# Whole strips for V in six one-layer steps at either end, half passes of 64 rows, and measured first times in the planner

## The chip, the core and the metric

The kernel runs on one core of a Trainium2 chip. Such a core has five engines with instruction queues of their own: TensorE (PE, matrix products; its weight loads are listed apart as PEld), VectorE (DVE), ScalarE (ACT), GpSimd (POOL) and SyncE (SP). SP and POOL also issue DMA transfers between the chip's memory and the core's on-chip memory. Work is ordered between engines with semaphores. The metric is the time of one execution on the device in microseconds; the number compared is the median over several executions.

## The reference

Two layers, each an attention with a recurrent memory followed by a gated feed-forward part, are applied twice with the same weights:

```python
x = x + A(layernorm(x)); x = x + B(layernorm(x))
x = x + A(layernorm(x)); x = x + B(layernorm(x))

def A(x):                               # 2048 rows of 512, 32 heads of 128
    mem = mem0                          # 8 rows
    for s in range(64):                 # segments of 32 rows, one after another
        h = concat(mem, x[32*s:32*s+32])            # 40 rows
        q, k, v = h @ Wq, h @ Wk, h @ Wv
        p = softmax(mask(q @ k.T * scale))
        o = (p @ v) @ Wo
        mem, out[s] = o[:8], o[8:]      # the first rows are the next segment's memory

def B(x):                               # F = 1792
    return (sigmoid(x @ w_gate) * (x @ w_up)) @ w_down
```

The memory makes the 64 segments of a layer a chain: segment s+1 can't start before the output projection of segment s is done. Inputs and outputs are bf16.

## The kernel before

Both attention layers run interleaved. Step t works on segment t of the first layer (j=0) and on segment t-6 of the second (j=1), side by side in one tile hT of 80 columns (`LAG` is 6). There are 70 steps. The first six have the first layer alone, the last six the second layer alone, with 40 columns; these are the one-layer steps. A feed-forward block works on four segments (128 rows, `BLK` is 4), and its pieces are spread between the attention work of the following steps.

One step (`emit_step`) goes through the 32 heads in six groups: Q and K (L834), a copy to on-chip memory by ACT, the scores (L848), the softmax on DVE and ACT (L862 to L879), transposes of P (L891), P times V (L914), and the output projection (L932), summed over all heads. Then DVE copies the new memory rows to the next step's hT (L945, L950), and ACT copies the rest to oxT, which L1002 transposes for the feed-forward block (L1034 gate and up, L1058 down).

V is not computed per step for all its rows:

- The rows of x of a segment that don't need the memory are known early. `v_pass` (L682) computes them for 128 rows at a time: 8 banks of 512 columns, four matmuls each, 32 matmuls of 128x512. The results go through a copy to the scratch tensor `scr` in the chip's memory. Before step 0 the first layer's passes come in groups (`v_group`), which is work for TensorE while the weights are loading. Later passes belong to the second layer and run after the feed-forward block that produces their rows; spare rows of those passes take up rows of the first layer (`v_fill`).
- The rows with the memory are computed in each step by `strips` (L759): 32 rows stand as a stationary tile of 32 columns, and four of them are put side by side in the array, 32 matmuls of 512 columns per strip.
- `emit_step` fetches both with SP DMAs into a tile `vsb`: L803 from `scr`, L814 from the strip's copy.

In the steps of `self.thin` a strip holds the memory and 24 rows of x, and only 8 rows come from `scr`. In the other steps 24 rows come from `scr` and the strip has the memory and 8 rows of x per layer. Before the change `thin` has four steps at either end; one-layer steps 4, 5, 64 and 65 are not in it.

The order of all instructions comes from a planner (`Planner`): every piece of work is a task with an engine, a duration, a latency, and keys that it reads and writes. `forward` runs through the tasks in a model of the engines, the PSUM banks and the DMA bus, and takes at each moment the ready task of highest priority. The priorities are not worked out in the kernel: they are a permutation written out as the string `SEQUENCE`. What is planned is emitted in order of planned start, engine by engine, so the planner's constants (`LAT`, `LEAD`, `TAIL`, `BUS`, `lat=`) and the string decide the instruction order, not the time at which an instruction runs on the chip. `warm` puts dummy matmuls (L1150) of a zero tile into planned holes of TensorE, so that its clock stays up; before `COLD` = 8000 ns of planned time it counts 1.2 columns per ns of the hole, after that 2.4. SP has eight DMA lanes: a DMA waits until the eighth one before it has landed. Large loads on POOL are also paced by TensorE's tasks.

At the start POOL clears tiles (L564 to L570), DVE and POOL normalise blocks of x (L638 to L642), TensorE transposes them (L651), and the first V matmul follows. Wv is loaded in five chunks of four or eight heads (L583), blocks of x between them (L721, L736).

Of the kernel before, what the change touches and what calls it, by code (L numbers as in the profile page):

```python
# [53 lines left out]
;AiJ8T3rAL|Nji^h>nE-)}}C6?#2*O0$8G4ZZdL%K2&sSfSGsr9F5bywiEpw1$9etJ{dj{n8$!UX!b>*%CVi0odWLR>PmMTURN8S`<`QSiresNn(7<<XH_|&hysZ(_+9io+E1yoPuJDs<%HrJ9~e&G  # L54
lO{?#YvSIBvP$R_;9f!1|GAlKk>X8^RhDlpmDnr7kt;6IZnSwn6|>@F3yW-VRO=#$!{s!|Z#sU*>kMf3XXFEnvc7`kKHK|1UA0@05#wb7a7HOlD?Yn#`J@z-(MeZ4Km`1|dy`f+^gMz@=%!FceG>$<
t$84$Kv|p6^^$~XKEw?)j1MY5bdV%#WrWw}B23to{C{XpW!a@PnfSMtcvtJ+x*0jL#Q{bGuEI}JeR4GK!d54vj>OKEncRQml~*<K;u1oaaQ4{bP`bof8*k|Jnvq^F=+Qyw{#`8!eH2|2^ft1nJbm7!
Ab!74vPh6M&l&LAlQ$kp(4RycR@9_lQx%SxC@=;7(#|M{pc-Zvq5^7mctV2pd4al%PqA<vseo$aQ(1$2O&p$$2=)#zF^2|o-u9XqFI-1Mc~jNaoYzdPrv`*zAA!u}T!KRNn7qKAo7WedWKFqAM5iWz
(lO=AI5ErprhTd6f)YVPYmhmHt`^X*krIWOe)K$vkW0fBn6t30v3~xgu9D9|2u?9Qhqxd3g!4-fxZSJdG?KXHi3=~m?P`o5>72)lIpD#^L81>xGR3Ji9|#WNB5L4{0_zR8rRp9-LS`%KDA3>to0^K8
trO%5X$z>-v_0tee?vxx^C`edFc{4p18&9J_1{77`WnlnpP=acza2)_2A~h&p}raH3Y3dS29jhXA=bf9kS8`f0IGrq5@}V)qI^z5??#c29baAb0B$86Cw+{B(m#uPRQTV>59ecM?f~YLiHK_agbl@M
>kXP60ej5O8Z1}7VtH~Tyi}o8Nh6os$k>dRMu$0U)mEux#MGAgPf!AyIq?@8yns1dXj`J(kB*bI#3S~kQG5MPNqKzX18+^sdBXNu6=5{T5Go1Hxs9?O$^vCQ9bSAntpCOL*N`Zy6d6f)8l}XGG}z!f  # L60
@(X9T<!k{a%zpTXjJr(t*vp+7A*WM2OF6JX&M0cCIFbCkn57sI8Q<FmQlDF2|3#N}6qtsBH%lb612z6V*1A9Y_A@HY$+fn$;9u1be-2ErQ~GLxg$2@V7S)+jTIXY3FAmgWqS`b0OT4UpsnQ7R$Uf33
f3q+HJ7f{+pc=}GM~NHQMP)4Ah>|J)wLO*-th<rKO_jdm{nOnoiY#EQdRE4_v%h|2_Nh`rzYRf!MHM6J(w85<_tb^)uriQo7uah{!`vFKpVnQ&1p}V2`ifjs&YA$@K)-I1;sCslWe)kvpEr4NIv$>b
$&(@1<pp8s;j>8S|K3v8wlu5u{sJg=#Rx9i+kw<LbAmj-UaSLL1MiR`VRCa!)$b@Ty6%s&&v4>}u`fQZ;+bdW<Ob3l-pr$_EMZQim=hbKvZ5di1HcO5lfzu>|J(t#K!!VbaFFOoH`q3<{|fuFn_mY>
# [90 lines left out]
class Task:  # L154
    __slots__ = ("eng", "dur", "lat", "fn", "deps", "succ", "tail", "boost", "ndep", "ready", "start", "idx", "on", "fresh", "acq", "rel", "durs", "tick", "prev", "land", "adj", "banks", "rate", "nb")

    def __init__(self, eng, dur, lat, fn, boost):
# [3 lines left out]
        self.acq, self.rel = [], []  # L161
        self.on = None
        self.land = 3000.0
        self.adj = {}
        self.banks = ()
        self.rate = 0.95
        self.nb = 0


class Buf:  # L170

    __slots__ = ("pool", "kind", "users", "first", "left", "slot", "t_free", "t_prev", "rd")

# [1048 lines left out]
```

## Time and profile before

| | |
|---|---|
| median of 4 runs | 1808.86 us (1807.73 to 1809.7) |
| the profiled execution, its own time | 1809.52 us |
| its span in the trace | 1807.8 us |
| busy: PE, DVE, ACT, POOL | 1771.7, 1152.5, 1189.5, 580.6 us |
| first V matmul of L682, first Q matmul of step 1 | 13.41, 89.07 us |
| end of the first six steps (the last copy of L950 before the two-layer steps) | 178.8 us |
| mean granted TensorE clock | 0.999 |
| data moved by DMA | 271.19 MB, mean 150 GB/s |

A row of the timeline reads: start, time from the first start to the last end of a merged group, engine, line, what it writes and reads, how many; in brackets the idle time of the engine before it and what ended it. Matmuls of TensorE overlap, so the price of one is the distance between starts and not its own duration. "L834 <- ACT qku" in the waits reads: the matmuls of line 834 waited for the ACT instruction that wrote qku. The chain that ended last is followed back from the last instruction; time on it is time that moves the end.

### The profile page before, as it was taken

The page shows a single profiled execution, that of the slowest core. Times are in us where ns is not written, and L with a number is a line of the kernel's source. Part 1 is how long each engine was busy: PE and PEld are TensorE (multiplying, and loading weights), DVE is VectorE, ACT ScalarE, POOL GpSimd, SP SyncE. Part 2 cuts the span into 40 slices and gives each one's busy share as a digit, 9 for nine tenths or more (in the row PEclk, how much of TensorE's full clock was granted, in tenths as well). Part 3 has the DMA queues.
Part 4 walks back from the last instruction along what each step waited for, and adds up shares of the span by engine and source line. Part 5 has one row for each costly group of instructions (what it writes and reads, how often), then busy time and mean ns, then how long its engine had stood idle before and what let it go on. Part 6 is the DMA issues. An engine that isn't in the chain of part 4 may idle for free.

```text
span 1807.8 us, 91891 instructions
## 1 busy us (share of the span) xinstructions
PE 1771.7 (98%) x39822; PEld 1524.9 (84%) x40039; DVE 1152.5 (64%) x3919; ACT 1189.5 (66%) x2987; POOL 580.6 (32%) x838
## 2 busy tenths in 40 slices
PE   9999999999999999999999999999999999999998
PEld 4588888988888888989898888988888888888886
DVE  4466665665566666665666667666666676566665
ACT  6666756676767666666766666666665666666664
POOL 6413032423233243323324241323334231332432
PEclk9999999999999999999999999999999999999999
DMA  9825254635455454445546463545556454554543
GB/s 344 274 71 151 58 150 117 192 110 155 141 160 151 131 169 142 142 129 160 159 128 197 129 179 91 167 139 163 153 145 178 120 142 119 157 153 126 178 124 109
DMA packets 136872, 271.19 MB, mean 150 GB/s; under 512 B 32650, under 2 KB 69138, under 8 KB 136466
## 3 DMA queue, kind: packets, MB, share of 16 engines
q0 software_dynamic: 56928, 184.07, 34.6%
q1 hardware_dynamic: 79538, 81.22, 15.7%
q8 instruction: 314, 5.14, 1.2%
q14 instruction: 92, 0.75, 0.1%
HBM read 220.93 MB, written 26.21 MB: 137 GB/s over the span
## 4 chain that ended last, share of the span: by engine, by line
PE 86%; DVE 7%; ACT 4%; issue 1%; POOL 1%; SPq 0%; ACTq 0%; DMA 0%; POOLq 0%; DVEq 0%
PE bank L834 30%; PE bank L932 15%; PE bank L1034 10%; PE bank L682 8%; PE bank L759 7%; PE bank L914 4%; PE bank L848 4%; PE bank L1058 4%; DVE st L862 2%; PE bank L891 2%; ACT ptsb L1158 1%; DVE small L867 1%; DVE small L874 1%; PE bank L651 1%; DVE st L869 1%
## 5 line engine op out<-in xcount | busy, mean ns | idle before, releaser
L834 PE MATMUL bank<-hT,wq_sb 128*128 128x80 bf16 (+1 forms) x8960 | 622.0, 198 | 0.9
L834 PE MATMUL bank<-hT,wk_sb 128*128 128x80 bf16 (+1 forms) x8960 | 621.9, 198 | 0.2 <-issue 0.2
L1158 ACT CAST qku<-bank 128x480 bf16<-128x480 f32 (+3 forms) x770 | 387.9, 513 | 220.0 <-PE bank L834 140.6
L834 PEld LDWEIGHTS <-wq_sb 128*128 128x128 bf16 x8960 | 454.9, 99 | 35.4 <-issue 22.1
L834 PEld LDWEIGHTS <-wk_sb 128*128 128x128 bf16 x8960 | 450.6, 99 | 0.1
L862 DVE TENSOR_TENSOR st<-bank,cst 40x240 f32<-40x240 f32 (+3 forms) x768 | 278.6, 367 | 233.0 <-PE bank L848 225.6
L932 PE MATMUL bank<-otsb,wo_sb 128*128 128x80 bf16 (+1 forms) x8960 | 363.3, 198 | 6.1 <-ACT otsb L1158 4.4
L932 PEld LDWEIGHTS <-wo_sb 128*128 128x128 bf16 x8960 | 338.0, 99 | 21.3 <-issue 8.1
L1026 POOL DMA_DIRECT2D wg<-in_B_w_gate_dram x217 | 164.4, 758 | 268.7 <-PE bank L1034 107.7
L1027 POOL DMA_DIRECT2D wu<-in_B_w_up_dram x217 | 163.9, 755 | 258.4 <-PE bank L1034 110.3
L1052 POOL DMA_DIRECT2D wd<-in_B_w_down_dram x217 | 153.7, 708 | 251.3 <-PE bank L914 82.4
L1158 ACT CAST otsb<-bank 128x480 bf16<-128x480 f32 (+3 forms) x420 | 198.0, 483 | 54.6 <-PE bank L914 40.8
L1158 ACT COPY ptsb<-bank 40x240 bf16<-40x240 bf16 (+3 forms) x559 | 177.9, 320 | 46.2 <-PE bank L891 36.5
L872 ACT ACTIVATE st<-st 80x240 f32<-80x240 f32 (+3 forms) x420 | 158.4, 381 | 43.5 <-DVE st L869 40.1
L1034 PE MATMUL bank<-xnT,wg 128*128 128x128 bf16 (+2 forms) x1784 | 171.5, 218 | 1.5 <-ACT xnT L1158 0.2
L1034 PE MATMUL bank<-xnT,wu 128*128 128x128 bf16 (+2 forms) x1784 | 171.0, 218 | 0.0
L874 DVE TENSOR_REDUCE small<-st 80x6 f32<-80x240 f32 (+3 forms) x420 | 151.3, 363 | 29.7 <-ACT st L872 27.3
L641 POOL TENSOR_TENSOR small<-small,cst 128x1 f32<-128x1 f32 (+1 forms) x80 | 45.2, 566 | 375.7 <-DVE small L640 357.4
L848 PE MATMUL bank<-qku 128*128 128x80 bf16 (+1 forms) x2240 | 160.5, 198 | 2.6 <-ACT qku L1158 1.5
L869 DVE TENSOR_TENSOR st<-st,small 80x240 f32<-80x240 f32 (+3 forms) x420 | 154.2, 369 | 3.5
L879 DVE TENSOR_TENSOR pb<-st,small 80x240 bf16<-80x240 f32 (+3 forms) x420 | 153.6, 369 | 4.1
L867 DVE TENSOR_REDUCE small<-st 80x6 f32<-80x240 f32 (+3 forms) x420 | 151.9, 363 | 4.5
(95 smaller groups left out, 2290.8 us busy)
## 6 DMA issues: line engine op xcount, KB each, us to landing
wg<-in_B_w_gate_dram POOLq DMA_DIRECT2D x220, 256.0 KB, 4.4
wu<-in_B_w_up_dram POOLq DMA_DIRECT2D x220, 256.0 KB, 4.3
wd<-in_B_w_down_dram POOLq DMA_DIRECT2D x220, 256.0 KB, 4.2
vsb<-scr SPq DMA_DIRECT2D x476, 48.0 KB
vsb<-sst SPq DMA_DIRECT2D x480, 32.0 KB
scr<-vst SPq DMA_DIRECT2D x120, 96.0 KB
wk_sb<-in_A_Wk_dram SPq DMA_DIRECT2D x10, 384.0 KB
wq_sb<-in_A_Wq_dram SPq DMA_DIRECT2D x10, 384.0 KB
```

Source lines behind the costliest of these rows:

```text
L834: nc.tensor.matmul(o_ap, lhsT=W[:, c, h * P:(h + 1) * P], rhs=mv(c), start=(c == 0), stop=(c == DC - 1))
L848: nc.tensor.matmul(s_all(SB)[:, w0 + i, :], lhsT=fview(qku[:, i, 0, 0:1], [(1, P)]), rhs=qku[:, i, 1, 0:ncol], start=True, stop=True)
L862: pl.add("DVE", dve_ns(n, True), lambda gsz=gsz, hs=hs, st=st, SB=SB, pj_=pj_, npj_=npj_, mk=mk, idx=idx: nc.vector.tensor_tensor(out=st[p ...
L867: pl.add("DVE", dve_ns(n), lambda hs=hs, st=st, mx=mx: nc.vector.tensor_reduce(out=mx[pr, hs], in_=st[pr, hs], axis=AX.X, op=ALU.max), r=s ...
L869: pl.add("DVE", dve_ns(n), lambda gsz=gsz, hs=hs, st=st, mx=mx: nc.vector.tensor_tensor(out=st[pr, hs], in0=st[pr, hs], in1=mx[pr, hs].uns ...
L872: pl.add("ACT", act_ns(n), lambda hs=hs, st=st: nc.scalar.activation(out=st[pr, hs], in_=st[pr, hs], func=ACTF.Exp, scale=self.scale), r=s ...
L874: pl.add("DVE", dve_ns(n), lambda hs=hs, st=st, sm=sm: nc.vector.tensor_reduce(out=sm[pr, hs], in_=st[pr, hs], axis=AX.X, op=ALU.add), r=s ...
L932: nc.tensor.matmul(WB[:, c * ncol:(c + 1) * ncol], lhsT=self.wo[:, h, c * P:(c + 1) * P], rhs=otsb[:, hl, 0:ncol], start=(h == 0 and c == ...
L1026: pl.add("POOL", 760, lambda wg=wg, fs=fs: nc.gpsimd.dma_start(out=wg[:], in_=self.wgv[:, :, fs]), r=[("wo", self.H - 1)], w=[gk] + bt, la ...
L1027: pl.add("POOL", 760, lambda wu=wu, fs=fs: nc.gpsimd.dma_start(out=wu[:], in_=self.wuv[:, :, fs]), r=[("wo", self.H - 1)], w=[uk] + bt, la ...
L1034: nc.tensor.matmul(gu[:, 2 * i + k, 0:n], lhsT=W[:, c, i * P:(i + 1) * P], rhs=xnT[:, c, rw], start=(c == 0), stop=(c == DC - 1))
L1158: nc.scalar.copy(out=dst, in_=src)
```

## The change

- `thin` goes from four steps at either end to six, which are all the one-layer steps. Steps 4, 5, 64 and 65 now take the memory and 24 rows from the strip and 8 rows from `scr`.
- So fewer rows are needed in `scr`. Of the first layer's blocks 0 and 1, block 0 needs 8 rows of each segment, and block 1 needs 8 rows of each segment and 16 more of two of them. One pass of 128 rows (`v_group([0, 1], ...)`) becomes one strip set (`v_strip`) and one half pass (`v_half`). For the second layer's block 14 (`b == NBLK - 2`) a pass becomes a half pass.
- `v_half` is new: 64 rows stand as a stationary tile of 64 columns, two beside each other in the array, 32 matmuls of 512 columns for all heads.
- At the program's start, blocks 2, 14, 3, 4, 5, 7 come ahead of mem0, block 0 and block 1.
- Wv is loaded in eight chunks of four heads, each after the chunk two before it has landed; the first chunk is issued before any block of x.
- The planner's constants change: a first time per engine (`FIRST`), lead times per queue, a slower bus in the first 18 us, and shorter latencies of transfers.
- A fourth buffer for the small results of the layernorm (`lns`).
- `SEQUENCE` is a new permutation, so the order of instructions differs on every engine and in nearly every step.

```diff
-    BUS, LEAD, TAIL, BIG, ROOM, POOL0 = 345.0, 2000.0, 1900.0, 300000, 1.0, 2000.0
+    BUS, BUS0, SLOW, BIG, ROOM, TAIL = 345.0, 290.0, 18000.0, 300000, 1.0, 1200.0
+    LEAD = {"SP": 1000.0, "POOL": 1800.0}
+    FIRST = {"PE": 0.0, "ACT": 2040.0, "DVE": 980.0, "POOL": 3500.0, "SP": 750.0}
...
-        free = {"PE": 0.0, "ACT": 0.0, "DVE": 0.0, "POOL": self.POOL0, "SP": 0.0}
+        free = dict(self.FIRST)
...
-                    bus = max(bus, now + self.LEAD) + tk.nb / self.BUS
+                    bus = max(bus, now + self.LEAD[e])
+                    bus += tk.nb / (self.BUS0 if bus < self.SLOW else self.BUS)
...
-        for h0, n in ((0, 4), (4, 4), (8, 8), (16, 8), (24, 8)):
+        for h0, n in ((0, 4), (4, 4), (8, 4), (12, 4), (16, 4), (20, 4), (24, 4), (28, 4)):
             cs = slice(h0 * P, (h0 + n) * P)
-            ld(self.wv[:, :, cs], wv_v[:, :, cs], P * self.DC * n * P * 2, [("wv", h) for h in range(h0, h0 + n)])
+            tk = ld(self.wv[:, :, cs], wv_v[:, :, cs], P * self.DC * n * P * 2, [("wv", h) for h in range(h0, h0 + n)], [("wv", h0 - 8)] if h0 > 4 else [])
+            if h0 > 4:
+                tk.after = pl.writer[("wv", h0 - 8)]
...
+    def take_part(self, pst, B, j, tile, keys, c0, r0, n, i0):
+
+        off = r0 + (MEM if j else 0) + SEG * i0
+        dst = fview(tile[:, 0, c0:c0 + 1], [(P, self.DC), (n, 2), (1, n)])
+        self.pl.add(("ACT", "DVE"), copy_ns(8 * n, True),
+                    lambda: (dst, fview(pst()[:, 0, off:off + 1], [(P, self.DC), (SEG, 2), (1, n)])), r=[B], w=keys)
+
+    def v_half(self, tile, c0, keys, j, b, q8, r16, i16, boot=False):
+        ...
+        for s in range(2):
+            vb = [pl.buf(self.bank, "v"), pl.buf(self.bank, "v")]
+            def mm(s=s, vb=vb):
+                for q in range(2):
+                    for c in range(DC):
+                        for i in range(2):
+                            k = 4 * s + 2 * i + q
+                            nc.tensor.matmul(vb[q][64 * i:64 * i + 64, :], lhsT=tile[:, c, c0:c0 + 64], rhs=self.wv[:, c, k * 512:(k + 1) * 512],
+                                             start=(c == 0), stop=(c == DC - 1), skip_group_check=True)
...
+    def v_strip(self, cols, keys, j, b, q8):
+        sb = self.strips(cols, keys)
...
-r=[("vd", j, b, q, kk) ...], w=[("vx", j, vh, i)], lat=5000.0, nb=nx * 2048)
+r=[("vd", j, b, q, kk) ...], w=[("vx", j, vh, i)], lat=4300.0, nb=nx * 2048)
...
-r=[(sb, 0), (sb, 1)], w=[(name, j, vh, i)], lat=3500.0, use=[sb], nb=nr * 2048)
+r=[(sb, 0), (sb, 1)], w=[(name, j, vh, i)], lat=3200.0, use=[sb], nb=nr * 2048)
...
+            if b == self.NBLK - 2:
+                self.take_v(pst2, B2, 1, self.xvl[q], [("xvl", q, 0)], 0, 16, 8)
+                self.take_part(pst2, B2, 1, self.xvl[q], [("xvl", q, 1)], 32, 0, 16, 0)
+                self.write_hT_x(pst2, B2, 1, BLK * b + self.LAG)
+                self.v_half(self.xvl[q], 0, [("xvl", q, 0), ("xvl", q, 1)], 1, b, 2, 0, 0)
                 return
...
-        self.thin = (range(BLK), range(self.NSEG - BLK, self.NSEG))
+        self.thin = (range(self.LAG), range(self.NSEG - self.LAG, self.NSEG))
...
-        p0 = self.pre1(0)
-        p1 = self.pre1(1)
...
-        self.load_mem0()
         self.load_weights()
...
-        self.v_group([0, 1], {0: p0, 1: p1}, [[(0, 96, 0, 8)], [(0, 0, 0, 24)]])
         self.v_group([2, 14], {}, [[(0, 0, 0, 24)], [(0, 96, 0, 8)]])
         self.v_group([3, 4, 5, 7], {}, cuts)
+        self.load_mem0()
+        p0 = self.pre1(0)
+        p1 = self.pre1(1)
+        x0 = self.xvl[2]
+        self.take_v(*p0, 0, x0, [("xvl", 2, 0)], 0, 0, 8)
+        self.v_strip(lambda c: x0[:, c, 0:32], [("xvl", 2, 0)], 0, 0, 0)
+        self.take_v(*p1, 0, x0, [("xvl", 2, 1)], 64, 0, 8)
+        self.take_part(*p1, 0, x0, [("xvl", 2, 1)], 96, 8, 16, 2)
+        self.v_half(x0, 64, [("xvl", 2, 1)], 0, 1, 0, 8, 2, True)
         self.v_group([8, 10, 11, 13], {}, cuts)
```

The latency of the feed-forward weights' loads goes from 5200 to 4700 in the same way. `v_half` ends with two copies and four DMAs per `s` to `scr`; `v_strip` ends with four DMAs.

## The prediction

> **What bounds the kernel now.** I read the page first (shares, then the chain that ended last), then the busy time by stretches of 5 us and of 100 us, then the timeline of TensorE in the head, TensorE's waits, and last the end of the chain.
>
> ```profile
> PE 1771.7 (98%) x39822; PEld 1524.9 (84%) x40039; DVE 1152.5 (64%) x3919; ACT 1189.5 (66%) x2987; POOL 580.6 (32%) x838
> PE 86%; DVE 7%; ACT 4%; issue 1%; POOL 1%; SPq 0%; ACTq 0%; DMA 0%; POOLq 0%; DVEq 0%
> ```
>
> TensorE is the bound: 98% busy, 86% of the chain. By stretches (start:end, then PE, PEld, DVE, ACT, POOL busy, clock, DMA share, GB/s):
>
> ```profile
> 5.00:10.00 5.00, 3.00 (x18) 1.16 (x16) 2.90 (x8) 1.30 (x4) 3.91 (x15) 0.96 0.93 305
> 40.00:45.00 5.00, 5.00 (x25) 2.29 (x24) 0.00 (x0) 3.20 (x6) 1.32 (x3) 1.00 1.05 366
> 100.00:105.00 5.00, 4.25 (x111) 3.40 (x108) 2.57 (x14) 2.95 (x11) 0.67 (x1) 1.00 0.24 69
> 1000.00:1100.00 100.00, 98.37 (x2238) 87.42 (x2249) 65.77 (x220) 65.63 (x161) 32.71 (x45) 1.00 0.52 150
> ```
>
> There are three stages. In the head, to about 80 us, TensorE and the DMA are both full. In the one-layer steps TensorE has holes, some of them stopped with dummy matmuls (L1150). In the two-layer steps TensorE is full and nothing else is near its limit. So V work taken out pays in the head and in the middle, and only partly in between. The head on the timeline, start and duration first:
>
> ```profile
> 1.00 5.44 PE L1150 MATMUL bank<-hot 128*128 128x512 bf16 x13 [1.00 <-DVE cst L557]
> ...
> 9.00 0.40 PE L651 MATMUL bank<-cst,xn 128*128 128x128 bf16 x4 [2.00 <-DVE xn L642]
> 9.23 3.21 PE L1150 MATMUL bank<-hot 128*128 128x512 bf16 x8
> ...
> 13.41 1.04 PE L682 MATMUL bank<-wv_sb,xvf 128*128 128x512 bf16 x4
> ...
> 60.81 2.75 PE L682 MATMUL bank<-wv_sb,xvf 128*128 128x512 bf16 x12
> 63.40 0.31 PE L848 MATMUL bank<-qku 128*128 128x40 bf16 x6
> ...
> 87.23 1.91 PE L759 MATMUL bank<-wv_sb,hT 128*32 128x512 bf16 x32
> 89.07 0.27 PE L834 MATMUL bank<-hT,wq_sb 128*128 128x40 bf16 x4
> ```
>
> Prices come from the distance between starts. A whole V matmul takes (63.40-60.81)/12 = 0.216 us. A strip matmul (32 columns, four side by side) takes (89.07-87.23)/32 = 0.0575 us. The first dummies take 0.43 us each: the array ran at half speed. Step 1 begins at 89.07. What TensorE waited for from 200 to 1600 us (us in total, times, longest):
>
> ```profile
> PE bank L1002 <- ACT oxT L1158: 4.6, 10, 0.5
> PE bank L932 <- ACT otsb L1158: 2.5, 6, 0.7
> PE bank L848 <- ACT qku L1158: 0.7, 2, 0.5
> ```
>
> No DMA stands there. The end of the chain, start and duration, dummies alone:
>
> ```profile
> 1792.02 0.38 PE bank L1150 x2
> ...
> 1792.77 0.92 PE bank L1150 x4
> ...
> 1794.37 0.27 PE bank L1150 x2
> ...
> 1796.00 0.48 PE bank L1150 x2
> ```
>
> **The change part by part.** The code's new SEQUENCE reorders every engine. I compared the instruction orders of the two programs.
>
> *V work.* 64 whole V matmuls go (13.8 us). In come 32 strip matmuls (1.84 us) and 64 half matmuls of 64 columns, two abreast. Nothing in the trace shows a half. Its ends are 0.108 (half of 0.216, perfect overlap) and 0.216 (none); I take 0.111, near the low end, because the strips overlap four ways at 0.0575 against an ideal 0.054. A use of 32 halves is then 3.55 us. In the head one pass (6.9) becomes a strip set and a half pass (1.84+3.55): -1.5. In the middle block 14's pass becomes a half pass: -3.4 (0 if the halves do not overlap).
>
> The Trainium skill, "TensorEngine Tiling (Array Packing)", Key Properties, speaks against this: changing the tiling mode drains the array. The strip rows hold such switches already, and 32 strips cost 1.84 against 32 x 0.054 = 1.73, so at most 0.11 a stretch. With four stretches of halves and two more sets of strips that rule would turn the sum below from -5.7 to about -5.1.
>
> *First dummies.* The program opens with 12.5 dummies of 512 columns now, with 31.5 after. They then separate three groups of transposes with 8.75, 3.75 and 2.75 more. The first V matmul follows. At 0.43 us until about 6.2 (in the trace the dummies are at full speed from 6.55) 12 run; the other 19.5 at 0.216 end at 10.4. Three transpose groups at 0.23 and 15.25 dummies at 0.216 (3.3) follow: V starts at 14.4, against 13.41. Ends: all 31.5 slow, 18.4; data first, 12.1 (the first normalised block can reach TensorE at about 8.1: two memsets of 0.44 fewer stand ahead of POOL's first L641, which starts at 7.34 now, 1.66 before its block is at TensorE).
>
> "TensorE: Matmul & The Clock Gate", Part 1, has the array at half clock until a free-running window of 3.4 us was busy. By it the turn falls between 4.4 and 7.8 us, the dummies end between 9.5 and 11.2 and V starts between 13.5 and 15.2. The trace agrees as to the size (slow to about 6.1), and shows a relapse to half clock at 10 to 13 us, after the 2.00 us wait, that the longer fill would avoid.
>
> *Rest of the head.* Between V's start and step 1 the order has 256 whole V matmuls now and 216 after: 32 are the pass that becomes strips and halves, and eight move past step 1's start. Work now: 55.3 V + 3.7 strips + 6.4 QK + 3.2 L932 + 2.0 scores, transposes and PV + 2.0 transposes of L651 + 0.7 dummies = 73.3, in 75.7 us, so 2.4 idle. After: 46.7 + 3.55 + 5.5 + 6.4 + 3.2 + 2.0 + 2.1 = 69.45, with the same idle 71.9. Step 1 begins at 14.4 + 71.9 = 86.3, that is **-2.8**, with ends -5.1 and +1.2 from V's start alone.
>
> This needs the weights in time. The load is the same (16.8 MB of weights, x, about 8 MB of V written), and the DMA runs at 366 GB/s from 10 to 70 us. Now the last L932 weights are issued by 75 us and used from 84. The cover is thus some 5 us, and the change uses 2.8 of it. SP's queue gets 19 more DMAs, POOL's 12 fewer; V writes now stand on SP from its 22nd DMA on, and each waits for an ACT copy with the weights of Wq, Wk and Wo queued behind it. Were the cover gone, the price is the 2.8. Wv's eight chunks wait for the second one before; SP's queue has a limit of eight in flight anyway, so this adds nothing that the queue didn't do.
>
> *One-layer steps.* Steps 4, 5, 64 and 65 fetch 8 rows instead of 24 from scratch and 32 instead of 16 from the strip, in the same number of strips, with as many DMAs. SP issues these, and TensorE doesn't wait for them now. Cost 0; ends -2.0 (dummies of steps 1 to 5 fall by that) and +1.7 (the eight V matmuls that moved there; they lie in holes: 4.25 of 5 us busy at 100).
>
> *Middle order.* Where the closing L932 of a step is followed at once by L1002, TensorE waits for ACT's oxT copy, up to 0.5 us. The order has 4 such places now and 7 after: **+1.5**. With the half pass the middle gives **-1.9**, ends -10 (all listed waits gone too) and +10 (below).
>
> *End.* After the last L932 1.8 us of dummies fall to 0.2, work of L1034 and L1058 in their place. They lie on the chain (2.05 us above), but what they wait for may stay: **-1.0**, between -2.0 and 0.
>
> Sum: -2.8 + 0 - 1.9 - 1.0 = **-5.7**. The profiled execution took 1809.5 (span 1807.8), 0.66 above the median of 1808.86. So 1803.8 by its own time and **1803.2** as a median. A difference within 0.2%, 3.6 us, is what a measurement here can't tell from none.
>
> **Rivals.**
> 1. *Slower: transfers planned too tight.* The plan now counts V reloads 0.7 us shorter (5.0 to 4.3), FFN weights 0.5, strips 0.3. The order may put the first PV of a step that much nearer to its reload. One place, L914 behind the vsb loads of L803, in 58 two-layer steps: more than 5.7/58 = 0.1 us a step takes the gain, 0.25 us a step gives +14.5-5.7, 1812. Against it: no DMA in TensorE's waits now, and the weights land in a median 4.4 us. Chance 0.16.
> 2. *The head pays nothing.* Dummies slow for longer, or V writes on SP hold the weights back: then -2.9 or less is left, 1806. Halves that do not overlap end here too (-5.7+6.7, 1810). Chance 0.20.
> 3. *Better than the sum.* The new order also removes the listed waits of the middle and the dummies of steps 1 to 5: -12, 1797. Against: its places with short cover are as many as before. Chance 0.14.
>
> **How the numbers follow.** The forecast has 0.50, with 1800 to 1806 as its own range. Faster by over 0.2% (below 1805.2): most of the forecast (0.44), rival 3, a little of rival 2: 0.61. Same: 0.06 of the forecast and most of rival 2: 0.23. Slower: 0.16. The range goes from just under rival 3 to the price of rival 1: 1795 to 1812.
>
> **What will show it.** The first L682 at 14 to 15 us; the first L834 of step 1 near 86; L682's whole matmuls 64 fewer and halves 0.11 us apart; L1002 waiting 6 to 7 us for oxT; about 0.2 us of dummies after the last L932. I am wrong if TensorE's waits name L914 with vsb transfers, if the head shows waits for weights, or if halves stand 0.216 apart.

## The result, and the profile after

The changed kernel takes 1813.06 us (median of 42 executions, 1809.92 to 1816.19) against 1810.3 for the kernel before (60 executions, 1807.67 to 1813.5). The ratio is 1.0015 with a 95% interval of 1.0011 to 1.0019. It is slower by 0.15%, which lies inside the 0.2% that the prediction called no difference, though the interval leaves no change out. The forecast of 1803.2 was faster by 0.31%. The measured time lies 9.9 us above it and 1 us above its range; 1.5 us of the 9.9 are the reference, whose median was 1808.86 us over 4 executions and is 1810.3 over 60.

The profiled execution took 1811.38 us, with a span of 1809.4 (before: 1807.8). The page's shares, then the chain that ended last:

```profile
PE 1770.8 (98%) x39846; PEld 1523.6 (84%) x40067; DVE 1164.2 (64%) x3931; ACT 1182.0 (65%) x2971; POOL 574.1 (32%) x826
PE 82%; DVE 7%; ACT 5%; issue 3%; DMA 2%; SPq 1%; POOL 1%; ACTq 0%; POOLq 0%; DVEq 0%
```

TensorE is the bound as before, at 98%. But its share of the chain fell from 86% to 82%, and DMA, which had 0%, has 2% (about 36 us). Four transfers of the head, before 61 us, make 25 of them: the chain now runs through transfers there. The same stretches as before (start:end, then PE, PEld, DVE, ACT, POOL busy, clock, DMA share, GB/s):

```profile
5.00:10.00 5.00, 5.00 (x24) 2.14 (x22) 3.29 (x8) 2.53 (x2) 2.62 (x8) 1.00 0.98 323
40.00:45.00 5.00, 4.81 (x25) 2.17 (x24) 0.00 (x0) 1.08 (x3) 0.00 (x0) 1.00 1.06 342
100.00:105.00 5.00, 4.74 (x127) 3.75 (x124) 4.26 (x20) 4.51 (x18) 1.11 (x2) 1.00 0.40 121
1000.00:1100.00 100.00, 98.33 (x2230) 87.32 (x2238) 66.79 (x226) 65.06 (x159) 33.85 (x47) 1.00 0.52 150
```

In the first row the clock reads 1.00 where it read 0.96: the kernel before fell back to half clock at 9.63 us, and this one did not. (The share covers only what is on record. The first clock record of this trace begins at 5.59 us, and before it the dummies start 0.43 us apart.) In the second ACT is busy for 1.08 us where it was busy for 3.20 us before, with TensorE still nearly full. The head on TensorE's timeline (start, duration, line, what, how many; in brackets idle time and what ended it). V's passes are now L690, halves L727, strips L812, Q and K L887, dummies L1210:

```profile
1.00 9.22 PE L1210 MATMUL bank<-hot 128*128 128x512 bf16 x32 [1.00 <-DVE cst L563]
...
14.16 1.90 PE L690 MATMUL bank<-wv_sb,xvf 128*128 128x512 bf16 x7
...
19.89 1.92 PE L727 MATMUL bank<-wv_sb,xvl 128*64 128x512 bf16 x16
21.75 0.60 PE L690 MATMUL bank<-wv_sb,xvf 128*128 128x512 bf16 x2
...
56.66 1.03 PE L690 MATMUL bank<-wv_sb,xvf 128*128 128x512 bf16 x4
61.00 7.48 PE L690 MATMUL bank<-wv_sb,xvf 128*128 128x512 bf16 x27 [3.32 <-ACT wg L1218]
...
88.81 1.91 PE L812 MATMUL bank<-wv_sb,hT 128*32 128x512 bf16 x32 [0.30 <-issue]
90.66 0.27 PE L887 MATMUL bank<-hT,wq_sb 128*128 128x40 bf16 x4
```

V starts at 14.16 where 14.4 was forecast. 16 halves take 21.75 - 19.89 = 1.86 us, so 0.116 apiece: two columns of the array do work side by side. Then TensorE stands for 3.32 us at 57.7, and the 27 matmuls after that take 7.48 us, where 27 at 0.216 would be 5.8: the granted clock is half from 60.21 to 63.62. Step 1 begins at 90.66 instead of the forecast 86.3, and 1.6 later than the 89.07 of before. TensorE's waits from 200 to 1600 us (us in total, times, longest):

```profile
PE bank L1055 <- ACT oxT L1218: 4.6, 11, 0.5
PE bank L985 <- ACT otsb L1218: 1.1, 5, 0.3
...
PE bank L901 <- ACT qku L1218: 0.5, 2, 0.3
```

L1055 (before L1002) waits as long as before, 4.6 us, and L985 (before L932) less. Nothing in this view accounts for a loss. At the end one dummy is left after the last output projection of L985, as forecast:

```profile
1792.02 0.96 PE L985 MATMUL bank<-otsb,wo_sb 128*128 128x40 bf16 x32
...
1796.22 0.33 PE L1210 MATMUL bank<-hot 128*128 128x384 bf16 x1
```

### Where the time came from

The ends of the same steps in the two profiles give the difference by stage. Each column but the forecast is one profiled execution, and each number says by how many us that stretch took longer than in the profile before. Stretches are named by their times in the kernel before. The columns from e2 on are kernels of the experiments below and stand here because all are read in the same way.

| stretch | forecast | after | e2 | e5 | e8 | e3 | e6 | e9 |
|---|---|---|---|---|---|---|---|---|
| head, to 87.1 | -2.8 | +1.0 | -3.6 | -4.1 | -2.8 | +2.6 | -3.9 | -4.5 |
| one-layer steps and three more, 87.1 to 256.6 | 0 | +1.5 | +2.4 | +3.8 | +2.5 | +3.5 | +3.8 | +1.0 |
| 256.6 to 1466.8 | +1.5 | +4.3 | +5.1 | +4.9 | +3.8 | +0.4 | +0.5 | -0.2 |
| 1466.8 to 1595.7 | | -0.9 | -0.9 | -0.8 | -0.9 | -0.3 | -0.3 | -0.4 |
| block 14, 1595.7 to 1695.6 | -3.4 | -2.3 | -2.4 | -2.1 | -2.3 | -0.9 | -1.7 | -2.1 |
| end, from 1695.6 | -1.0 | -1.9 | -1.0 | -1.9 | -1.8 | -0.1 | +0.4 | -1.5 |
| sum | -5.7 | +1.7 | -0.4 | -0.2 | -1.5 | +5.2 | -1.2 | -7.7 |

Three terms failed: the head, the one-layer steps and the middle. The experiments take them in turn. A profile is one execution. That of the kernel before is 0.8 us faster than its median, that of the changed kernel 1.7 faster, that of e2 1.2 slower. e4 and e10 below keep the head of the kernel before and still stand at +1.0 and +0.9 there, with half clock for 6.83 us where its profile has 3.41. So the columns tell where time goes, to about 1 us in the head, and the ratios below tell how much in all.

### The stall in the head

The wait of L690 at 57.7 is for ACT (a copy to the buffer wg). ACT's waits from 10 to 90 us, and its timeline at the two places:

```profile
ACT wg L1218 <- DMA scr<-wg: 6.8, 1, 6.8
ACT wu L1218 <- DMA scr<-wu: 5.7, 1, 5.7
```

```profile
36.88 1.31 ACT L1218 CAST wd<-bank 128x512 bf16<-128x512 f32 x2
43.92 0.59 ACT L1218 CAST wu<-bank 128x512 bf16<-128x512 f32 x1 [5.73 <-DMA scr<-wu]
...
52.93 0.59 ACT L1218 CAST wg<-bank 128x512 bf16<-128x512 f32 x1 [0.28 <-PE bank L690]
60.37 0.59 ACT L1218 CAST wg<-bank 128x512 bf16<-128x512 f32 x1 [6.85 <-DMA scr<-wg]
```

In the kernel before, ACT's waits over the same stretch name a write out of a staging buffer only once:

```profile
ACT wg L1158 <- DMA scr<-wd: 0.3, 1, 0.3
```

In the head V's results go to `scr` through staging buffers. The idle weight buffers wd, wg and wu serve as nine of them, 1024 columns each, filled in two halves by two groups of matmuls and copies. ACT waits here for the earlier write out of the same buffer: the one behind 60.37 was issued at 53.49 and landed at 60.27. The banks of TensorE fill up behind ACT until it stands as well.

The plan did not see this. `Planner` counts a buffer as taken from its first-listed user (`T[bf.users[0]].acq.append(bf)`), which is the first half's group. For these two buffers the sequence runs the second half's group first, 11.0 and 12.6 us ahead in planned time. So on the chip the buffer is wanted that much earlier than the plan believes, before the write out of it can have landed.

### The profile page after: what moved, and what is told of

The parts are those of the page before. It is cut to its first block, busy times and chain, and to the rows that moved or that the text cites. A ratio compares the mean times of both kernels' runs of the same rounds, so it can differ in the third digit from the quotient of the medians.

```text
span 1809.4 us, 91920 instructions
## 1 busy us (share of the span) xinstructions
PE 1770.8 (98%) x39846; PEld 1523.6 (84%) x40067; DVE 1164.2 (64%) x3931; ACT 1182.0 (65%) x2971; POOL 574.1 (32%) x826
## 4 chain that ended last, share of the span: by engine, by line
PE 82%; DVE 7%; ACT 5%; issue 3%; DMA 2%; SPq 1%; POOL 1%; ACTq 0%; POOLq 0%; DVEq 0%
PE bank L887 29%; PE bank L985 15%; PE bank L1087 9%; PE bank L812 7%; PE bank L690 6%; PE bank L967 4%; PE bank L901 4%; PE bank L1111 3%; PE bank L944 2%; ACT ptsb L1218 2%; DVE st L915 1%; ACT qku L1218 1%; DVE small L927 1%; PE bank L1210 1%; DVE small L920 1%
## 5 line engine op out<-in xcount | busy, mean ns | idle before, releaser
L887 PE MATMUL bank<-hT,wq_sb 128*128 128x80 bf16 (+1 forms) x8960 | 622.1, 198 | 0.7 <-issue 0.2
L887 PE MATMUL bank<-hT,wk_sb 128*128 128x80 bf16 (+1 forms) x8960 | 621.8, 198 | 0.1
L887 PEld LDWEIGHTS <-wq_sb 128*128 128x128 bf16 x8960 | 454.5, 99 | 35.9 <-issue 24.7
L887 PEld LDWEIGHTS <-wk_sb 128*128 128x128 bf16 x8960 | 450.6, 99 | 0.2
L985 PE MATMUL bank<-otsb,wo_sb 128*128 128x80 bf16 (+1 forms) x8960 | 364.8, 198 | 3.7 <-ACT otsb L1218 1.9
L985 PEld LDWEIGHTS <-wo_sb 128*128 128x128 bf16 x8960 | 339.0, 99 | 21.8 <-issue 5.8
L1218 ACT COPY ptsb<-bank 40x240 bf16<-40x240 bf16 (+3 forms) x577 | 182.5, 318 | 40.9 <-PE bank L944 30.8
L649 POOL TENSOR_TENSOR small<-small,cst 128x1 f32<-128x1 f32 (+1 forms) x80 | 44.6, 559 | 410.4 <-DVE small L648 410.0
L932 DVE TENSOR_TENSOR pb<-st,small 80x240 bf16<-80x240 f32 (+3 forms) x420 | 154.0, 370 | 4.9
```

Source lines behind the costliest of these rows:

```text
L887: nc.tensor.matmul(o_ap, lhsT=W[:, c, h * P:(h + 1) * P], rhs=mv(c), start=(c == 0), stop=(c == DC - 1))
L985: nc.tensor.matmul(WB[:, c * ncol:(c + 1) * ncol], lhsT=self.wo[:, h, c * P:(c + 1) * P], rhs=otsb[:, hl, 0:ncol], start=(h == 0 and c == ...
L1218: nc.scalar.copy(out=dst, in_=src)
```

## The experiments

Each ratio is against runs of the kernel before in the same session, whose median was 1811.9 us for e1 to e4, 1811.79 for e5 to e8 and 1810.02 for e9 and e10. So the ratios can be compared with each other and with the 1.0015 of the changed kernel, and the times of different sessions cannot.

Two theories stood against each other for the head: SP's queue (the prediction's rival 2, writes of V that hold weights back) and the staging buffers. For the middle the question was whether its order or something carried over from the head costs the time.

### e1: writes of V on the other queue

All of the head's V writes and loads that may go on either queue go to POOL, so that none stands on SP ahead of weights.

```diff
-                    {"SP": nc.sync, "POOL": nc.gpsimd}[tk.on].dma_start(out=got[1], in_=got[2])
+                    (nc.gpsimd if len(tk.durs) > 1 else nc.sync).dma_start(out=got[1], in_=got[2])
```

> The changed kernel with one edit: all V writes of the head (L1214) go on POOL's queue, so that no weight on SP stands behind a write that waits for ACT. Queue theory: in the changed kernel SP issued nothing from 41.9 to 47.0 us, the DMA fell from about 360 to 140-310 GB/s for 8 us (about 1.1 MB, 3 us of transfer), and that is the 3.3 us for which TensorE stands at 57.7. Then the stall falls under 1 us, the half-clock window behind it (1.4 us) goes too, step 1 starts at 86 to 87 instead of 90.7, and the time falls by 3.5 to 4.5 us against the changed kernel, to about 1.5 us under the kernel before. Rival, staging: ACT has nine staging buffers and each is held until its write has landed, 5 to 7 us later; then the queue makes no difference, ACT still waits for a write, TensorE stands for 2.5 us or more, and the time is within 1 us of the changed kernel's.

Measured: 1816.53 us, ratio 1.0024 (1.0015 to 1.0033), so no faster than the changed kernel. ACT's waits and TensorE's waits of e1 from 10 to 90 us, and two windows of its head:

```profile
ACT wg L1218 <- DMA scr<-wg: 9.7, 1, 9.7
ACT wu L1218 <- DMA scr<-wu: 6.9, 1, 6.9
```

```profile
PE bank L690 <- ACT wg L1218: 4.2, 1, 4.2
PE bank L659 <- DVE xvf L1220: 1.9, 1, 1.9
PE bank L659 <- ACT wu L1218: 1.3, 1, 1.3
```

```profile
56.00:60.00 4.00, 2.14 (x16) 1.12 (x14) 1.66 (x3) 0.00 (x0) 3.21 (x6) 1.00 1.07 381
60.00:64.00 4.00, 0.20 (x1) 0.10 (x1) 0.11 (x1) 0.28 (x1) 0.00 (x0) 0.72 1.07 391
```

In these two windows the transfers do not pause: the DMA moves 381 and 391 GB/s while TensorE is idle for most of the second. So SP's queue was not what held the head. In the changed kernel SP issues nothing from 41.85 to 46.98 us; with ACT's wait gone, in e2, its longest hole around there is 0.7 us. So that hole follows from ACT's wait. With the writes on POOL the waits for the buffers grow from 5.7 and 6.8 to 6.9 and 9.7 us.

### e2: twelve staging buffers in place of nine

The same order on every engine, replayed, with three more buffers of 1024 columns. They are made of tiles that are idle in the head (th, xnT, vst).

```diff
-        self.xnT = [c.tile([P, DC, P], BF16, name=f"xnT{i}") for i in range(1)]
+        xvm = c.tile([P, 1, 1024], BF16, name="xnT")
+        self.xnT = [xvm[:, 0, 0:512].rearrange("p (c n) -> p c n", c=DC)]
...
-        self.bootp = Pool([fview(w[:, 0, 0:1], [(1, 1024)]) for w in self.wd + self.wg + self.wu])
+        self.bootp = Pool([fview(w[:, 0, 0:1], [(1, 1024)]) for w in self.wd + self.wg + self.wu + [thm, xvm, vsm]])
```

> The changed kernel with its own order of instructions on every engine, but twelve staging buffers for the V copies of the head instead of nine (the three come from buffers that the FFN uses only from 180 us on). Staging theory: ACT's 6.9 us wait for a landed write at 53.5 falls under 2 us, TensorE's stall of 3.3 us and the half-clock window behind it go, step 1 starts at 86 to 87, 3.5 to 4.5 us are saved against the changed kernel. Queue theory: SP's gap at 42 to 47 and the low DMA rate come from writes that wait on ACT; with ACT free earlier the gap may shrink, but the weights are as many and the stall stays above 2 us.

Measured: 1808.05 us, ratio 0.9976 (0.9966 to 0.9985). The stretch where the changed kernel stood, and the start of step 1, on TensorE's timeline of e2 (V's passes are L612 and Q and K L809 in it):

```profile
56.70 7.20 PE L612 MATMUL bank<-wv_sb,xvf 128*128 128x512 bf16 x31
...
86.03 0.27 PE L809 MATMUL bank<-hT,wq_sb 128*128 128x40 bf16 x4
```

The 4 + 27 matmuls run through without a stop, ACT's longest wait for a write is 0.4 us, and step 1 begins at 86.03. The forecast for the head was 86.3.

### e5: the two halves next to each other

Nine buffers again. For the two buffers alone, the late group of matmuls and its copies are moved in the written order so that both halves come one after the other. (Told in words here; in the code the string `SEQUENCE` changes.)

```diff
 order of the two groups of a buffer in the head
-wu, second half  ...  (11.0 us)  ...  wu, first half
-wg, second half  ...  (12.6 us)  ...  wg, first half
+wu, first half, second half
+wg, first half, second half
```

> The changed kernel with nine staging buffers, one edit in the order: the two V matmul groups that fill the second half of a staging buffer 11.0 and 12.6 us (in the plan) ahead of the group that fills its first half go to just before that group, with their ACT copies. The plan counts a buffer as taken only from the group of its first half on, so it gave each of these two buffers to the early group 8.3 us before the last write from it lands. Theory: these two are ACT's waits of 5.7 and 6.8 us for landed writes at 38.2 and 53.5 us, and the second is what stops TensorE; with the pairs together both waits fall under 1.5 us, the 3.3 us stall and the half-clock window go, and the time is 3 to 5 us under the changed kernel's, as with twelve buffers (perhaps 1 us less, since the later groups now come a place earlier than their data). Rival: nine buffers are too few at this rate of V work whatever the order; then ACT's waits on landed writes stay above 3 us each and the time is within 1.5 us of the changed kernel's.

Measured: 1808.74 us, ratio 0.9984 (0.9976 to 0.9993). No wait of ACT for a write is longer than 0.5 us, TensorE has no wait of 0.2 us or more from 14 to 90 us, and step 1 begins at 85.20 (timeline of TensorE in e5):

```profile
85.20 0.27 PE L806 MATMUL bank<-hT,wq_sb 128*128 128x40 bf16 x4
```

More buffers and a better order with the old number of buffers both remove the stall. So its cause is the buffer wanted too early, and not the memory or the load of the DMA.

### e8: the first dummies as short as before

e2, with the first row of dummies cut back to what the kernel before has.

```diff
                     B, n = fill[tk.idx]
+                    if tk.start < 9000.0:
+                        n = min(n, 50)
```

> The changed kernel with twelve staging buffers, and the first run of dummy matmuls cut from 31.5 to 12.5 (as many as the kernel before has). The first normalised block is ready at 9.9 us and the dummies end at 10.06, so the V matmuls can start at most 0.2 us earlier. Theory: TensorE idles from about 6.4 to 9.9, the clock falls to half for a window of 3.4 us from 9 or 10 us on as in the kernel before (9.6 to 13.0), and the first V work is slowed: 0.5 to 1.7 us lost, step 1 later by as much. Rival: the clock stays or the loss is taken up by waits for data at 12 to 14 us: no change within 0.5 us.

Measured: 1808.75 us, ratio 0.9983 (0.9974 to 0.9992), against 0.9976 (0.9966 to 0.9985) for e2: the difference lies inside the intervals. In the profiles V starts later, at 15.52 instead of 14.75. The timeline of TensorE in e8:

```profile
10.07 0.61 PE L581 MATMUL bank<-cst,xn 128*128 128x128 bf16 x4 [3.75 <-DVE xn L572]
...
15.52 1.68 PE L612 MATMUL bank<-wv_sb,xvf 128*128 128x512 bf16 x7
```

Without the longer fill TensorE is idle for 3.75 us, and the granted clock is half from 9.41 to 12.82 us. In e8 the data set the time of the first transposes (10.07). In the changed kernel DVE had the block ready at 9.86 us and the transposes followed the dummies at 10.06, so the longer fill delays them by 0.2 us at most and saves the relapse of the clock. At the end of step 0 the two profiles are 0.8 us apart.

### e3: the middle of the kernel before

The changed kernel, with the instruction order of the kernel before from 250 to 1480 us. The order is replayed task by task. The older constants apply in that stretch, and `lns` has 12 rows so that no new wait comes in.

```diff
-    MID = (0.0, 0.0)
+    MID = (245000.0, 1480000.0)
...
-        self.lns = [small[:, 10 * i:10 * i + 10] for i in range(4)]
+        self.lns = [small[:, 10 * i:10 * i + 10] for i in range(12)]
```

> The changed kernel, with the instructions of all engines from 250 to 1480 us (steps 8 to 56, about 9200 of 13292 planned tasks) in the order that the kernel before has; head and end stay the changed kernel's. (The layer-norm scratch has 12 rows instead of 4, which takes away false dependences between the two orders.) Theory: between 250 and 1480 us the changed kernel fell back by about 3.5 us (from 2.5 to 6.0 behind), with no single wait to show for it, because its order has thinner cover in many places; with the old order the step lengths from 250 to 1480 are those of the kernel before within 0.7 us in sum, and the time is 3 to 4 us under the changed kernel's. Rival: the drift comes with the shifted transfers or the chip's state, not with the order; then the time stays within 1 us of the changed kernel's.

Measured: 1811.56 us, ratio 0.9996 (0.9987 to 1.0005) against 1.0015 (1.0011 to 1.0019) of the changed kernel. Its one profile is a poor one: 1814.78 us, with half clock for a second stretch at 183 us and for longer at 60 us, which is why its head and one-layer steps stand so high in the table. Its middle is what was asked for: +0.4 from 256.6 to 1466.8, where the changed kernel has +4.3.

### e6: twelve buffers and the middle of before

Both edits, e2 and e3, together.

> Twelve staging buffers and the order of the kernel before from 250 to 1480 us, in the changed kernel. If the two faults are independent the gains add: 4.0 us under the kernel before with the buffers alone, and 3.4 us between the changed kernel with and without the old middle order, so 7 to 8 us under the kernel before, a ratio of 0.9955 to 0.9965. Rival: with the head earlier, the middle's transfers come at other moments and the arrears return; then the ratio is 0.997 or above.

Measured: 1806.88 us, ratio 0.9973 (0.9962 to 0.9983). The middle is +0.5. With e9 below there are three profiles with the old middle (+0.4, +0.5, -0.2) and five with the new one: the changed kernel, e2, e5 and e8 in the table, and e1 with +5.3. These five have +3.8 to +5.3, whatever their head did. So the new order of the middle costs some 4.4 us by itself, and nothing carried over from the head does. (The old order came with 12 rows of `lns` in these runs, and the new order was not run with 12. The kernel before has the old order with three.)

No single place holds the loss. The total of TensorE's busy time over the stretch rises by 4.0 us (1193.45 of 1210.2 before, 1197.42 of 1214.5 after) with the same number of matmuls (26735 and 26734), and its idle time by 0.3. A matmul's modelled duration is about 0.2 us (198 ns for L887, whose starts stand 36 ns apart) and runs past the start of the next one, so a hole shorter than that counts as busy. The loss is therefore in many holes below 0.3 us, and the table of waits hardly sees it. The distances between starts show where the holes sit. Within runs of matmuls of one kind (Q with K, gate with up) they add up to 1021.8 us before and 1020.2 after. At the changes from one kind to another, 2070 before and 2069 after, they add up to 188.1 and 193.9, and e9 with the old order is back at 188.1. The largest part stands ahead of P times V, which comes 1.9 us later in sum (1.3 in e2). The wait for oxT, the one that the prediction priced, is 3.4 us in this stretch against 3.0 before.

Yet e6 is not as fast as its parts promise. It lost in the one-layer steps. TensorE's timeline in e6, and two windows of it (start:end, PE, PEld, DVE, ACT, POOL busy, clock, DMA share, GB/s):

```profile
174.37 0.46 PE L908 MATMUL bank<-otsb,wo_sb 128*128 128x40 bf16 x12
176.20 0.40 PE L582 MATMUL bank<-cst,xn 128*128 128x128 bf16 x4 [1.38 <-DVE xn L573]
...
177.17 3.60 PE L735 MATMUL bank<-wv_sb,hT 128*32 128x512 bf16 x32
```

```profile
173.81:177.22 3.41, 1.99 (x57) 1.53 (x57) 1.37 (x5) 1.27 (x7) 2.18 (x4) 1.00 0.56 162
177.22:180.63 3.41, 3.41 (x32) 1.20 (x32) 0.72 (x3) 1.16 (x5) 1.90 (x3) 0.50 0.69 177
```

TensorE waits 1.38 us for a normalised block of x (xn). The 32 strips behind it take 3.53 us (177.17 to 180.70) instead of 1.84, at half clock. The changed kernel has the same wait at 180, without the half clock after it. Its POOL and TensorE:

```profile
175.69 0.71 POOL L1105 DMA_DIRECT2D wd<-in_B_w_down_dram  x1 [0.78 <-PE bank L1111]
178.58 0.73 POOL L1105 DMA_DIRECT2D wd<-in_B_w_down_dram  x1 [2.18 <-PE bank L985]
179.34 0.58 POOL L649 TENSOR_TENSOR small<-small,cst 128x1 f32<-128x1 f32 x1
```

```profile
178.59 0.46 PE L985 MATMUL bank<-otsb,wo_sb 128*128 128x40 bf16 x12
180.42 0.40 PE L659 MATMUL bank<-cst,xn 128*128 128x128 bf16 x4 [1.37 <-DVE xn L650]
```

L649 is the layernorm's power on POOL, one small operation of 0.58 us. Ahead of it in POOL's queue stands a load of w_down, and that load is paced: it waits 2.18 us for a matmul of L985. So the layernorm, and with it TensorE, waits for a transfer that can come later, as e9 shows. In the kernel before, the same power (L641 at 176.89) also stood behind loads, of which the last four did not wait for TensorE, and TensorE waited 0.5 us at this place:

```profile
PE bank L651 <- DVE xn L642: 0.5, 1, 0.5
```

### e9: the power ahead of the paced load

e6, with that one load of w_down moved behind the power in POOL's order (again told in words).

```diff
 POOL, end of step 5
-wd load of L1028 (paced by TensorE)
 layernorm power of L572
+wd load of L1028 (paced by TensorE)
```

> The kernel with twelve staging buffers and the old middle order (ratio 0.9973), with one DMA issue moved in POOL's queue: the reload of wd (L1106 in the changed kernel) that waits until TensorE has done a given L985 matmul at 174 us now stands behind the layer norm's power step (L649), not ahead of it. In the run without the move POOL waited 2.2 us for TensorE with that DMA in hand, the power step ran at 175.1 though its input was there at 173.5, and TensorE waited 1.4 us for xn at 176; right behind it the clock stood at half for 3.4 us. Theory: the 1.4 us wait shrinks to 0.3 or less, the half-clock window goes with it, step 6 is reached 1.3 to 3 us earlier, and the ratio falls to 0.9957 to 0.9967. Rival: the DMA that now comes later, or DVE, delays something else by as much; then 0.9970 or above.

Measured: 1801.71 us (five executions, 1800.1 to 1803.76) against 1810.02, ratio 0.9955 (0.9941 to 0.9969). This is faster than both kernels, by 8.3 us against the one before. Against e6 the intervals of the ratios still overlap (0.9962 to 0.9983 there), so what the moved load is worth is read from the traces. POOL, TensorE and the chain of e9:

```profile
173.35 0.56 POOL L572 TENSOR_TENSOR small<-small,cst 128x1 f32<-128x1 f32 x1 [1.45 <-DVE small L571]
```

```profile
174.09 0.46 PE L908 MATMUL bank<-otsb,wo_sb 128*128 128x40 bf16 x12
174.41 0.40 PE L582 MATMUL bank<-cst,xn 128*128 128x128 bf16 x4
...
175.38 1.91 PE L735 MATMUL bank<-wv_sb,hT 128*32 128x512 bf16 x32
```

```profile
PE 86%; DVE 8%; ACT 4%; issue 2%; SPq 0%; DMA 0%; POOL 0%; ACTq 0%; DVEq 0%; POOLq 0%
```

The power now waits only for its input, the transposes follow the output projection without a stop, the strips run at full clock, and TensorE has its 86% of the chain again, with DMA at 0%. In the stretch of the one-layer steps e9 stands at +1.0 against +3.8 of e6: the 1.4 us of wait and the 1.7 of half clock are gone (3.1; the profiles differ by 2.8).

### e4, e7 and e10: the half pass

e4 keeps the kernel before up to 1430 us, head included, and has the half pass of block 14, the thin steps and the end of the changed kernel.

```diff
-    MID = (0.0, 0.0)
+    MID = (-1.0, 1430000.0)
...
-        for h0, n in ((0, 4), (4, 4), (8, 4), (12, 4), (16, 4), (20, 4), (24, 4), (28, 4)):
+        for h0, n in ((0, 4), (4, 4), (8, 8), (16, 8), (24, 8)):
```

> The kernel before up to 1430 us, and the changed kernel's tasks and order from there: the half pass for block 14, whole strips for the last six one-layer steps, and the end. My prediction's own terms for these are -3.4 for the half pass and -1.0 for the end, -4.4 together; read from the changed kernel, which went from 6.0 behind at 1520 us to 1.7 behind at the end, it is -4.3. So 1805.5 to 1806.5, a ratio of 0.9975 to 0.998. Rival: what the changed kernel made up there was only its own arrears (holes that its order had left); then the gain is under 2 us.

Measured: 1807.86 us, ratio 0.9977 (0.9966 to 0.9987). This is the part of the change that pays without any repair. Block 14's stretch gives -2.1, the changed kernel's own -2.3.

e7 is e4 with the two column halves issued one after the other, four matmuls each, instead of in turn.

```diff
-                    for c in range(DC):
-                        for i in range(2):
+                    for i in range(2):
+                        for c in range(DC):
```

> The kernel before up to 1430 us with the changed kernel's end, as run above (ratio 0.9977), and one edit in the half pass of block 14: all four matmuls of the first 64 columns, then the four of the second 64, where the kernel alternates between the two. The changed kernel's halves stand 0.116 us apart where alternating. Theory: two halves overlap only when they follow each other, so the 32 matmuls go from 0.116 to about 0.216 us apart and cost 3.2 us, a ratio of 0.9990 to 1.0000. Rival: the spacing doesn't depend on the order; no change from 0.9977 (within 0.0008).

Measured: 1807.74 us, ratio 0.9978 (0.9969 to 0.9987), the same as e4. The spacing is 0.117 us against 0.116. The overlap does not depend on alternating the halves in the program.

e10 is e4 with the half pass computed twice, the second time over the first, which adds 32 halves.

```diff
-                for q in range(2):
+                for q in (0, 1, 0, 1):
```

> The kernel before up to 1430 us with the changed kernel's end (ratio 0.9977); the 32 matmuls of block 14's half pass are done twice over (the second time over the first, same result), 3.7 us of TensorE's work more by the measured 0.116 us. It prices V work at this place. The half pass took 3.2 us of work away, but the kernel moved ahead there by only 1.5 us. Theory: V work here lies partly over holes (it hides chains of DVE and ACT), so 3.7 us of it cost about half, 1.5 to 2.2 us between 1595 and 1696 us. Rival: TensorE has no holes here, the doubled work costs all of its 3.7 us, and what the half pass didn't bring was lost to an order with worse cover.

Measured: 1808.89 us, ratio 0.9993 (0.9984 to 1.0002). TensorE's timeline of e10, with one of the two rows of halves and what follows it:

```profile
1612.71 3.64 PE L643 MATMUL bank<-wv_sb,xvl 128*64 128x512 bf16 x32
1616.29 0.60 PE L893 MATMUL bank<-otsb,wo_sb 128*128 128x80 bf16 x12
```

32 halves take 1616.29 - 1612.71 = 3.58 us. Adding 32 of them cost 3.5 us between 1595.7 and 1695.6 (+1.4 against -2.1 of e4). By the ratios it is 0.0016, or 2.9 us. So V work added there is paid for in full, or nearly, and work taken out should pay in full too. A whole pass in place of 32 halves would be 6.9, and 6.9 - 3.6 = 3.3 us were taken out. Most profiles show 2.1 to 2.6 of them in this stretch (e6 1.7, e3 0.9). By this sum about 1 us is lost in other places of the new order there. One is to be seen in TensorE's waits of the changed kernel from 1595 to 1696, and it is not in those of the kernel before:

```profile
PE bank L944 <- DVE pb L932: 0.7, 1, 0.7
```

## Why the prediction was wrong

**V work and halves: right.** The half was put at 0.111 us between 0.108 and 0.216. The rows show 0.112 to 0.116. The Trainium skill, "TensorEngine Tiling (Array Packing)", Key Properties, has a change of tiling mode drain the array. 16 halves took 1.86 us against 16 x 0.108 = 1.73, so at most 0.13 us a stretch goes there, much like the 0.11 bounded from the strips. e10 bears this out: 32 halves in one stretch took 3.58 us, so the second 16 cost 1.72, or 0.108 apiece, and the rest falls once a stretch.

**V's start: right, with some luck.** 14.16 against 14.4, and 13.54 to 14.75 in e1, e5, e2 and e9 with the same instructions ahead of it. The prediction had the first normalised block at TensorE at about 8.1. DVE finished it at 9.86, 0.2 us before the dummies ended.

**Rest of the head: its work right, its cover wrong.** Where the stall is taken away, step 1 begins at 86.03 (e2), 85.20 (e5) and 84.80 (e9). The forecast of 86.3 is thus the right sum of work. The step that failed is "the cover is thus some 5 us, and the change uses 2.8 of it", with "were the cover gone, the price is the 2.8" as its bound. The cover looked at was that of the weights in SP's queue. What gave way was the reuse of the staging buffers: ACT's copies wait up to 6.8 us for the write before, and TensorE loses 3.3 us standing and some 1.6 us at half clock. The price of lost cover was +3.8 and not 2.8 (from -2.8 to +1.0), and from e2's -3.6 it is 4.6. The prediction's "each waits for an ACT copy with the weights of Wq, Wk and Wo queued behind it" followed the chain in one direction only: the ACT copies wait in turn for earlier writes to land, and that wait was put at nothing. Of rival 2 the outcome for the head came true (it pays nothing), but not the mechanism, as e1 shows.

**One-layer steps: the cost of 0 failed**, though +1.5 lies inside the ends given. The step looked at SP's fetches, and TensorE shows no wait for them in these steps. It did not go through POOL's queue, where a paced load had come to stand ahead of the layernorm's power: 1.4 us of wait where the kernel before has 0.5, and in some executions 1.7 us of half clock behind it. e9 shows both, by moving one instruction. This explains only part of the row. By steps, the changed kernel lost 1.0 us in step 4 and 0.7 in step 5, where that wait is. e9 lost 0.3 in step 1, where the V matmuls that moved past its start are, and 0.7 in step 4, and the cause in step 4 stays open.

**Middle: the sign of the new order was right, its size and place wrong.** Forecast were +1.5, for three more places where L1055 waits for oxT, with 6 to 7 us in that row. The row shows 4.6 us, as before. The new order cost 4.3 us from 256.6 to 1466.8 all the same, spread over holes at the changes between kinds of matmul that are too short for the table of waits, and e3, e6 and e9 lose it by going back to the old order. This is 0.09 us for each of the 47 steps there (6016 matmuls of Wq, 128 a step). Counting the places of one known wait could not find it.

**Rival 1 did not happen.** The only wait of L967 (before L914) for a vsb transfer in the whole run is 0.2 us, once. Shorter planned transfers did no harm there. Its price was also added up wrongly: +14.5 - 5.7 is +8.8, which from 1808.86 gives 1817.7 and not 1812. The range took its upper end from there, so by the prediction's own terms it should have reached 1817.7, and 1813.06 would have lain inside, though not by that rival's mechanism.

**Half pass of block 14 and the end: nearly right.** -2.3 against -3.4: the size of the gain from the halves is right, and about 1 us was lost beside it. The end gives -1.9 in the changed kernel against -1.0, with dummies of one matmul left as forecast. The profiles that share this end lie between -1.9 and +0.4 (e7, with half clock for 3.4 us from 1708.7, at +1.8), so a single one does not size it.

The sum of the terms that the change itself buys (head, block 14, end) was close to right, and e9 reaches it: -8.3 us, with the stalls mended and the old order in the middle. The prediction went wrong in what the new order costs elsewhere. It was put at +1.5, and it was +3.8 in the head, +1.5 in the one-layer steps and +3.4 from 256.6 to 1595.7.

## What to carry to other kernels

When a plan or a scheduler reorders work, go through every buffer with more than one writer and ask which writer comes first, and whether the plan counts the buffer as taken from that one; a stall on a reused buffer shows as an engine that waits for a DMA out of it, far ahead of the wait on the engine that matters. On a queue that issues paced transfers and also does small operations, look at what stands directly behind each paced transfer: one instruction moved took 1.4 us of wait and 1.7 us of half clock out of the trace here. And a change of work should be tried with as much of the old order as can be kept: the same work was worth -0.45% with the old order in the middle and the two stalls mended, and +0.15% with the order that came with it.

## What the runs showed of the hardware that was not expected

- The granted clock changes on a fixed grid of 3.41 us. With the same first instructions from 1.00 us on, it turned to full at 3.77 us (e1), 5.31 (e9), 5.59 (the changed kernel) and 6.78 (e2), and V's start followed at 13.54, 13.86, 14.16 and 14.75. "TensorE: Matmul & The Clock Gate", Part 1, in the Trainium skill tells of such a free-running window of about 3.4 us; the traces agree. In e1, however, 2.77 us of work in a window of 3.41 were enough for the turn. So were 2.62 in the changed kernel (60.21 to 63.62), and 2.53 in e4 (8.12 to 11.53) were not.
- Much less than an idle window brings half clock back. In e6 one window with 1.42 us idle (1.99 busy of 3.41) was followed by half clock for 3.41 us. In the changed kernel the same wait of 1.37 us falls across the border of two windows, and the clock stays full. The same page gives one idle window as the condition, and here the measurement decides. The phase of the window is not all of it: in e5 and in e2 the whole 1.37 us lie in one window (172.78 to 176.19 and 174.03 to 177.45), and the clock fell in e5 and stayed full in e2. So about 1.4 us of idle time in one window is near the border, and whether such a wait costs 1.4 or 3.1 us differs between executions.
- Two column halves of the array overlap as well when four matmuls of one half are issued before four of the other (0.117 us apiece in e7, 0.116 in turn).
- A higher transfer rate did not make the awaited writes land earlier. From 56 to 64 us e1 moved 381 and 391 GB/s, the changed kernel 367 and 306, and yet ACT waited longer for its writes in e1 (6.9 and 9.7 us against 5.7 and 6.8).
